# Hand-written table of order: another order, engine choice and set of slots for the same 1,474 nodes

## The chip, the cores and the metric

The kernel runs on one core of a Trainium2 chip. Five engines work side by side: TensorE (PE, with weight loads shown as PEld), VectorE (DVE), ScalarE (ACT), GpSimd (POOL) and SyncE (SP, which here only issues transfers). Each runs its own instructions strictly in order. Sixteen DMA engines move the data that SP, POOL and ACT ask for.

The metric is the device time of one execution in microseconds (us). Before the change it is 289.76 us, the median of three runs (289.59 to 290.92).

## What is computed

Two stages. A linear attention with a feature map of 128 features per sign, for 8 batches, 8 heads, 576 rows and 64 columns a head, and then a feed-forward layer of three products, their maximum, and an output product on 4608 rows:

```python
def phi(x):
    proj = np.einsum('bhsd,df->bhsf', x, w_phi)
    proj = proj - np.max(np.abs(proj), axis=-1, keepdims=True)
    return np.concatenate([np.exp(proj), np.exp(-proj)], axis=-1)
q_p, k_p = (phi(q), phi(k))
kv = np.einsum('bhsf,bhsd->bhfd', k_p, v)
z = np.sum(k_p, axis=2)
num = np.einsum('bhsf,bhfd->bhsd', q_p, kv)
den = np.einsum('bhsf,bhf->bhs', q_p, z)[..., None] + 1e-06
...
h = np.maximum(np.maximum(x @ w1, x @ w2), x @ w3)
return (h @ w_out).astype(np.float32)
```

All inputs and the output are float32 in memory. On the chip the products take bf16.

## The kernel before

**Units.** The attention is cut into 16 units of four heads; two units make one batch. `attention(u)` makes the nodes of one unit, a node being a few instructions of one engine with the nodes that it needs, the buffers that it uses and the function that issues it:

- `L`, `Lv`: loads of q, k and v. Units 0 to 3 load q and k as bf16 through POOL's queue (L449), except for unit 0, whose q and k come in halves as float32 through SP's (L435) and are cast on DVE or ACT (L442). All others load 576 KB each through SP's queue (L460) and are cast on POOL (`C`, L466).
- `T`: q and k of a unit side by side, turned so that columns become partitions (`qkT`). Units 0 to 3 do this on PE with an identity (L480) and copies (`Tc`, L483). Units 4 to 15 do it with one transposing transfer in SP's queue (L495).
- `G`: `psq` and `psk`, the products of `qkT` with the feature weights (L518). They use 64 of PE's rows each, two at a time. Five batches a unit: four of four tiles, one of two. `ek` (ACT, L531) and `r` (DVE, L537) read them.
- `R`, `mT`, `V`: the maxima of q's rows turned on PE (L545), copied (L549), and sent as one more row into `qkT` by a small transfer (L553) from SP's or ACT's queue. Units 0 and 1 do without.
- `M` (L597) and `eq` (L610): the same products for q, transposed, less the maxima, and their exponentials.
- `E`, `va`, `vd` (L568, L572, L582): the exponentials of k's maxima, multiplied into v and beside it.
- `K` (L626): keys by values, 72 matmuls on 64 rows each; `kv` copies the sums (L631). `N` (L644) and `x` (L650, L651): the queries' products and the division.
- `X`: the result turned into `xT`. Units 0 and 1 on PE (L664, L667), the others with a transposing transfer in SP's queue (L674).

**Feed-forward.** `chunk(b, ...)` takes 512 of a batch's 576 rows; a ninth chunk takes the 64 left over from all eight. `up` and `up2` are groups of four matmuls of 512 columns (L697), evacuated by `t1` (ACT L705 or DVE L707) and `h` (DVE L703). `down` is a group of four (L725) and one of six (L730), evacuated by `osb` (L738) into one of four buffers and stored through SP or, in the ninth chunk, ACT (L745). Some nodes at the start prepare products of the weights (`wd`, `wt`, `we`, `wm`, `mo`).

**Order.** Nothing is scheduled while the program is built. `plan` reads a long string, `PLAN`. A word such as `756S0@146.2` says: node 756 goes to SP (T is PE, D is DVE, A is ACT, G is POOL), it takes slot 0 of its buffer, and a planner, which is not part of the kernel, meant it to start at 146.2. The order of the words is the order in which the nodes are issued, so each engine's order follows from it, and the slots say which tile or PSUM bank a node has to wait for.

**Idlers.** The planned starts have one use: where PE's plan has a gap, `fill` puts matmuls into it that use constants and write to a free bank (L827, `idler`).

Of the kernel before, what the change touches and what calls it, by code (L numbers as in the profile page):

```python
# [104 lines left out]
139A@25.0 167D@25.2 165D@25.5 1088T2@25.6 138A@25.6 50G@25.6 1090T1@26.0 124A1@26.1 1089D@26.3 112A@26.3 127G0@26.5 140T5@26.5
70T167@26.7 125G@26.7 1091A@26.8 99D@27.4 111A@27.7 126G@27.9 1096T2@27.9 72D@28.2 141A@28.2 71A@28.5 104D@28.5 142A@28.7
120A@29.3 173T106010@29.3 1097A@29.6 122G@29.6 183T51@29.6 1094T7@29.9 176D@29.9 174A@30.1 187D@30.5 186D@31.1 184A@31.2
73T31@31.3 75T4@31.6 175A@31.7 160D3@31.7 74D1@31.8 128T5@31.9 161S@31.9 1082G@32.1 1095A@32.1 134T6@32.4 362S1@32.4 76D0@32.4
185A@32.6 297S0@32.8 79T2@32.8 135A@33.1 178T47@33.2 80D0@33.4 131T3@33.5 136A@33.7 426S0@33.8 177D@34.0 77T2@34.2 121G@34.2
133A@34.3 1098T6@34.5 181D@34.6 129A@34.8 229D2@35.2 132A@35.3 78D1@35.3 123G@35.3 1080G@35.6 168T01@35.8 182D@35.9 1099A@36.0  # L110
143T032@36.1 171D@36.5 130A@36.5 179A@37.0 172D@37.1 188T60@37.3 231T5@37.4 144A@37.5 192D@37.7 145A@37.8 170A@38.1 191D@38.1
148T20@38.2 232D0@38.4 1092T4@38.5 196A1@38.5 190A@38.7 198G1@38.9 169A@39.0 149D1@39.0 189A@39.5 152T6@39.8 1093A@40.1
83T0@40.1 153D1@40.4 235T5@40.4 180A@40.6 146T4@40.7 197G@41.0 236D@41.0 84A@41.0 81T6@41.1 147D0@41.3 193T5@41.5 150T7@41.5
199A@41.7 233T1@41.8 82A@41.8 194D1@42.0 151D0@42.2 195S@42.3 154T4@42.4 234D@42.8 242T012601@42.8 230S@43.0 365G@43.1 155A@43.1
237T07@43.2 156T5@43.4 245D@43.4 296S1@43.5 238A@43.7 215T143@43.9 157D@44.0 366S1@44.4 246D@44.5 252T51@45.0 241D@45.1
1104T2@45.2 217A@45.2 1083G@45.3 216A@45.5 240D@45.7 253A@45.8 1112T4@46.2 239A@46.3 255D@46.3 1105A1@46.7 256D@46.9 247T03@47.0
1085G@47.4 257T27@47.4 1110T5@47.5 250D@47.6 249A@47.6 248A@48.2 260D@48.2 203T01@48.5 1102T2@48.7 1111A@48.7 251D@48.8
254A@49.2 1081G@49.5 1116T5@49.5 259A@49.7 1103D@49.8 243A@49.9 363S1@50.3 209T1@50.4 205A@50.4 1114T2@50.6 1117D@50.7
557S1@50.7 211A@50.9 261D@51.3 244A@51.4 1124T5@51.5 299G1@51.6 1113D@51.6 204A@51.9 210A@52.3 200T6@52.4 212T4@52.6 1125D@52.6
1122T3@52.7 1084G@52.7 213A@52.9 202A@53.2 1115D@53.2 262T0@53.5 1108T5@53.6 265A1@53.7 1123D@53.8 263A1@53.9 214A@54.1  # L120
264S@54.3 258A@54.4 387T111010@54.5 367T32@54.7 1109A@54.7 429G0@54.8 382T47@54.9 390D@54.9 428S0@55.0 201A@55.2 1120T5@55.3
# [4 lines left out]
392T7@63.1 278T2@63.3 285D@63.3 374A@63.4 222T5@63.5 393D0@63.7 220T1@63.8 430G@63.9 378A@63.9 376D@64.0 394S@64.0 1126T7@64.1
279A@64.4 286D@64.6 298S2@64.7 395A0@64.8 223D1@64.9 272T6@65.0 280A@65.1 275T0@65.2 396G1@65.2 287T40@65.4 273A@65.5 431S0@65.6
1127T@65.7 288D1@66.0 276A@66.0 274A@66.5 221D0@66.6 277A@67.0 307T013201@67.2 397G@67.3 302T46@67.4 1128A1@67.5 289T1@67.6
310D@67.7 291T5@68.0 304A@68.1 305D@68.2 1134T7@68.4 308A@68.5 292D0@68.8 303A@69.0 408T31@69.2 560G1@69.4 1135T@69.5 311D@69.5
226S@69.5 410A@69.7 290D0@70.1 309A@70.2 559G@70.5 409A@70.6 306D@70.7 293T4@70.8 317T12@71.1 1136A3@71.1 294D1@71.3 322T06@71.4  # L130
312T53@71.5 398G@71.6 324A@71.8 1138T7@71.9 320D@71.9 318A@72.1 295S@72.1 325D@72.5 319A@72.6 402T4@72.7 624G0@72.8 316D@72.9
411T1@73.0 1139T@73.1 403A@73.2 315D@73.5 323A@73.7 404A@74.0 491S1@74.0 321D@74.1 414T050@74.4 412A@74.4 326D@74.7 313A@74.7
1140D0@75.0 330A1@75.2 314A@75.4 332G0@75.5 399T2@75.6 416D@75.8 415A@75.9 405T6@75.9 442T003710@76.1 400A@76.1 561S1@76.3
# [725 lines left out]
```

## Time and profile before

| | |
|---|---|
| median of three runs | 289.76 us (289.59 to 290.92) |
| the profiled execution: its time | 290.44 us |
| its span, first to last instruction | 288.7 us |
| granted TensorE clock | 1.000 |
| moved by DMA | 51.45 MB, 178 GB/s on average |
| transposing transfers of `qkT` | 12, SP's queue held 2.7 to 6.2 us each |

A row of the chain of waits gives start, length and what the time went to: an engine with a line of the kernel, or a transfer on which the next instruction waited. A row of a timeline gives start, duration, engine, line, operation and tiles; brackets at its end hold the idle time of the engine just before it and what ended it. A row of the groups has the count, the busy time, the mean duration in ns, and the idle time before the group. A row of the windows gives, behind the stretch and its length, the busy time and the count of PE, PEld, DVE, ACT and POOL, the granted clock, the share of the DMA engines that was busy, and GB/s. PE's matmuls overlap in their pipeline, so the durations of single ones add up to more than the time they take together.

### The profile page before, as it was taken

The page shows a single profiled execution, that of the slowest core. Times are in us where ns is not written, and L with a number is a line of the kernel's source. Part 1 is how long each engine was busy: PE and PEld are TensorE (multiplying, and loading weights), DVE is VectorE, ACT ScalarE, POOL GpSimd, SP SyncE. Part 2 cuts the span into 40 slices and gives each one's busy share as a digit, 9 for nine tenths or more (in the row PEclk, how much of TensorE's full clock was granted, in tenths as well). Part 3 has the DMA queues.
Part 4 walks back from the last instruction along what each step waited for, and adds up shares of the span by engine and source line. Part 5 has one row for each costly group of instructions (what it writes and reads, how often), then busy time and mean ns, then how long its engine had stood idle before and what let it go on. Part 6 is the DMA issues. An engine that isn't in the chain of part 4 may idle for free.

```text
span 288.7 us, 8634 instructions
## 1 busy us (share of the span) xinstructions
PE 279.6 (97%) x3587; PEld 155.0 (54%) x3587; DVE 204.9 (71%) x431; ACT 197.8 (69%) x456; POOL 121.8 (42%) x104
## 2 busy tenths in 40 slices
PE   8999999998999999999998999999999999999994
PEld 3466675465565655556455466565544654444452
DVE  3978888897999787967788778897976362156210
ACT  2799898998989998886896978977664501330021
POOL 8048969949517159564552634062162000000000
PEclk9999999999999999999999999999999999999999
DMA  7999979999989999999999988869400037610064
GB/s 184 275 251 209 236 280 205 283 309 210 178 208 257 254 262 238 246 213 272 209 231 226 257 177 201 210 136 143 82 4 0 2 75 144 139 30 0 6 157 130
DMA packets 68193, 51.45 MB, mean 178 GB/s; under 512 B 48762, under 2 KB 52922, under 8 KB 68154
## 3 DMA queue, kind: packets, MB, share of 16 engines
q1 hardware_dynamic: 63759, 45.55, 66.6%
q0 software_dynamic: 4000, 4.92, 9.9%
q8 instruction: 28, 0.46, 0.7%
q10 hardware_dynamic: 395, 0.43, 0.4%
q14 instruction: 11, 0.09, 0.1%
HBM read 34.64 MB, written 9.44 MB: 153 GB/s over the span
## 4 chain that ended last, share of the span: by engine, by line
PE 75%; DMA 15%; ACT 5%; DVE 2%; SPq 1%; issue 1%; ACTq 0%
PE ups L697 29%; PE ops L730 13%; DMA qkT<-qk_bf 9%; PE ops L725 9%; PE psn L644 5%; PE psq L518 5%; PE kvps L626 4%; PE psm L597 4%; DMA k_raw<-in_k_dram 2%; ACT Eq L610 2%; DMA xT<-x_sb 2%; PE pm L796 2%; ACT Ek L531 2%; DMA qkT<-mT 1%; DVE mqp L537 1%; PE idler L827 1%
## 5 line engine op out<-in xcount | busy, mean ns | idle before, releaser
L697 PE MATMUL ups<-xT,w_bf 128*128 128x512 bf16 x432 | 102.0, 379 | 0.2
L610 ACT ACTIVATE Eq<-psm 128x512 bf16<-128x512 f32 (+1 forms) x160 | 80.4, 575 | 18.6 <-PE psm L597 17.6
L531 ACT ACTIVATE Ek<-psk 128x512 bf16<-128x512 f32 (+1 forms) x160 | 81.8, 574 | 9.8 <-PE psk L518 7.3
L572 POOL TENSOR_TENSOR vab<-v_raw,em 128x1152 bf16<-128x1152 f32 (+1 forms) x35 | 67.2, 1929 | 50.2 <-ACT em L568 44.5
L697 PEld LDWEIGHTS <-w_bf 128*128 128x128 bf16 x432 | 40.2, 98 | 44.7 <-issue 0.4
L537 DVE TENSOR_REDUCE mqp<-psq 128x4 bf16<-128x512 f32 (+1 forms) x80 | 49.0, 633 | 10.8 <-PE psk L518 7.8
L537 DVE TENSOR_REDUCE mk<-psk 128x4 f32<-128x512 f32 (+1 forms) x80 | 49.4, 630 | 4.6 <-PE psk L518 2.7
L730 PE MATMUL ops<-wout_bf,hT 128*128 128x512 bf16 (+1 forms) x222 | 51.5, 373 | 0.0
L703 DVE TENSOR_TENSOR hT<-hT,ups 128x512 bf16<-128x512 bf16 x54 | 35.8, 682 | 11.9 <-PE ups L697 10.0
L738 ACT COPY osb<-ops 128x512 f32<-128x512 f32 (+1 forms) x21 | 12.2, 586 | 30.8 <-PE ops L730 13.4
L651 DVE TENSOR_TENSOR x_sb<-psn,rden 128x320 bf16<-128x320 f32 x64 | 31.5, 492 | 2.2
L644 PEld LDWEIGHTS <-Eq 128*128 128x128 bf16 x640 | 26.8, 97 | 11.4 <-DVE x_sb L651 0.4
L730 PEld LDWEIGHTS <-hT 128*128 128x128 bf16 x222 | 20.8, 98 | 21.2 <-DVE hT L703 0.2
L705 ACT ACTIVATE hT<-ups 128x512 bf16<-128x512 f32 x33 | 19.6, 607 | 18.1 <-PE ups L697 16.9
L644 PE MATMUL psn<-kv_sb,Eq 128*128 128x65 bf16 x640 | 29.3, 194 | 0.3 <-DVE x_sb L651 0.3
L738 DVE COPY osb<-ops 128x512 f32<-128x512 f32 (+1 forms) x16 | 10.7, 670 | 25.4 <-PE ops L730 12.7
L518 PE MATMUL psq<-w,qkT 64*128 64x128 bf16 x288 | 24.1, 217 | 2.7 <-DMA qkT<-qk_bf 2.6
L518 PEld LDWEIGHTS <-qkT 64*128 64x128 bf16 x576 | 16.5, 94 | 16.2 <-issue 9.6
L725 PE MATMUL ops<-xT 128*128 128x512 bf16 x96 | 24.5, 379 | 0.0
L518 PE MATMUL psk<-w,qkT 64*128 64x128 bf16 x288 | 24.1, 217 | 0.0
L466 POOL CAST qk_bf<-k_raw 128x1152 bf16<-128x1152 f32 x12 | 13.7, 1146 | 22.7 <-DMA k_raw<-in_k_dram 22.7
L597 PE MATMUL psm<-qkT,wphi_m 128*128 128x512 bf16 (+1 forms) x70 | 21.8, 358 | 0.3 <-DMA qkT<-mT 0.3
(71 smaller groups left out, 245.2 us busy)
## 6 DMA issues: line engine op xcount, KB each, us to landing
v_raw<-in_v_dram SPq DMA_DIRECT2D x16, 576.0 KB, 5.5
out_dram<-osb SPq DMA_DIRECT2D x65, 128.0 KB, 2.5
q_raw<-in_q_dram SPq DMA_DIRECT2D x12, 576.0 KB, 7.0
k_raw<-in_k_dram SPq DMA_DIRECT2D x12, 576.0 KB, 6.0
w_bf<-in_moe_w_dram POOLq DMA_DIRECT2D x3, 768.0 KB, 14.7
qk_bf<-in_q_dram POOLq DMA_DIRECT2D x3, 288.0 KB, 12.6
qk_bf<-in_k_dram POOLq DMA_DIRECT2D x3, 288.0 KB, 11.9
wout_bf<-in_moe_w_out_dram POOLq DMA_DIRECT2D x1, 768.0 KB, 20.9
```

Source lines behind the costliest of these rows:

```text
L518: nc.tensor.matmul(ps()[:, i, :], lhsT=cols[r, :], rhs=w2[r, c, :], start=True, stop=True)
L531: nc.scalar.activation(Ek[s]()[:, tiles_of(t0, n), :], of(1), EXP, scale=1.0 - 2.0 * s)
L537: nc.vector.tensor_reduce((mq, mk)[c]()[:, tiles_of(t0, n)], of(c), AXX, ALU.max, apply_absolute_value=True)
L572: (nc.vector if n_.eng == "DVE" else nc.gpsimd).tensor_tensor(vab()[:, g, t0:t1, 0:D], vb()[:, t0:t1, :], em()[:, g, t0:t1].unsqueeze(2).t ...
L597: nc.tensor.matmul(psm()[:, 0:w], lhsT=wphi_m, rhs=rhs, start=True, stop=True)
L610: nc.scalar.activation(Eqb()[s][:, cols], psm()[:, 0:w], EXP, scale=1.0 - 2.0 * s)
L644: nc.tensor.matmul(psn()[:, c, :], lhsT=Eqb()[g][:, t0:t0 + P], rhs=kv()[:, pr, ab, g, :], start=(g == 0), stop=(g == 1))
L651: nc.vector.tensor_tensor(x_sb()[:, pr, :, ab, :], psn()[:, :, 0:D], rden().to_broadcast([P, 5, D]), ALU.mult)
L697: nc.tensor.matmul(ups(), lhsT=w_bf[i + 1][:, ct, j * P:(j + 1) * P], rhs=tokens_of(ct), start=(ct == 0), stop=(ct == CT - 1))
L703: nc.vector.tensor_tensor(hT()[:, j, :], hT()[:, j, :], ups(), ALU.max)
L725: nc.tensor.matmul(ops_()[:, 0:width], lhsT=tile_of(ct, tt), rhs=line_w[c_i > MOVE][:, ct, cols], start=(ct == 0), stop=False)
L730: nc.tensor.matmul(ops_()[:, 0:width], lhsT=hT()[:, j, tt * P:(tt + 1) * P], rhs=wout_bf[:, j, cols], start=False, stop=(j == JT - 1))
```

## The change

The string `PLAN` is replaced by another one. All other lines stay: the nodes, what each computes, the dependences, the buffers and their numbers. What differs is the order of the words, the engine letter of 80 nodes (of those that may run on more than one), slots, and the planned starts. The number of idlers in the program goes from 43 to 34. On PE the order changes between matmuls on 64 rows (`G`, `K`) and on 128 rows 75 times before and 81 times after; four of the six more lie ahead of the first `up`.

The words of the nodes that the prediction speaks of, and of some near them:

| nodes | what | words before | words after |
|---|---|---|---|
| 10, 6 | first halves of unit 0's k and q, loads | 10S1@0.7 6S0@1.1 | 10S1@1.1 6S0@0.7 |
| 9, 14 | casts of the second halves of unit 0's q and k | 9A@7.4 14A@9.1 | 9D@6.8 14D@8.6 |
| 361 | load of unit 5's q | 361S0@8.2 | 361S1@2.8 |
| 88 | load of unit 1's v | 88S@14.7 | 88S@24.1 |
| 1087 | copy of the first turned w1 tile | 1087D1@19.0 | 1087A1@18.7 |
| 50, 123 | columns of ones-times-em (`vd`) of units 0 and 1 | 50G@25.6 123G@35.3 | 50A0@17.8 123A@34.3 |
| 195, 589, 784, 914, 979 | `V` of units 2, 8, 11, 13, 14 | 195S@42.3 589S@103.6 784A@169.8 914S@152.7 979S@195.2 | 195A@40.7 589A@103.4 784S@171.4 914A@155.8 979A@210.3 |
| 301, 691, 756 | `T` of units 4, 10, 11 | 301S2@59.7 691S1@117.9 756S0@146.2 | 301S2@58.6 691S0@119.6 756S1@148.0 |
| 719 | `V` of unit 10 | 719S@144.0 | 719S@147.1 |
| 297, 296, 426 | loads of unit 4's k, q and unit 6's q | 297S0@32.8 296S1@43.5 426S0@33.8 | 297S1@38.1 296S1@32.9 426S0@32.0 |
| 1459, 1460, 1463, 1464 | the last full `down` and its copy out | 1459T@280.2 1460A2@281.8 1463T@275.9 1464A1@277.5 | 1459T@278.5 1460D1@280.0 1463T@282.0 1464D2@283.5 |

SP's order around three transposing transfers, before and after (a letter and the unit; `L` is a load of q or k):

```
T4   before: Lv5 L8 V3 Lv6 L9 L8 L6 T4 V5 Lv4 T6
     after:  L8 Lv3 Lv5 V3 Lv6 Lv4 L6 T4 L9 L8 V5 T6
T10  before: store1 store1 X6 store1 Lv9 T10 L11 L11 V9 T13
     after:  store0 store1 V7 X6 store1 T10 Lv9 L12 L11 V9 T13
T11  before: L15 store2 X8 store2 L12 V10 Lv13 T11 L14 V13
     after:  Lv12 L15 L15 X8 Lv13 V10 T11 store2 store2 L12 X9
```

The diff replaces the whole string; these are lines that hold words of the table:

```diff
...
-158G@4.5 1079G@5.2 7A@5.7 1G@6.0 16T5@6.4 1077G@6.5 17D2@7.2 9A@7.4 27T103510@7.9 361S0@8.2 22T27@8.2 30D@8.4 31D@9.0 14A@9.1
...
-115T012701@14.6 88S@14.7 58T30@14.7 118D@15.0 117A@15.0 61T5@15.3 41D@15.3 59A@15.5 64T2@15.8 48D1@15.9 38A@16.0 89T6@16.3
...
+2D7@0.7 4A@0.7 0G@0.7 6S0@0.7 3D@1.1 10S1@1.1 85G1@1.2 8S@1.5 13S@2.0 86G@2.0 15S1@2.4 361S1@2.8 1076G@2.9 7A2@3.6 1G@3.6
...
+1088T1@23.1 163D2@23.2 107A@23.4 67T6@23.6 87D1@23.8 117A@23.9 137T70@24.0 109D@24.0 88S@24.1 101A@24.1 70T134@24.5 1089D@24.6
...
-371D@58.9 266G@59.1 427S0@59.3 208A@59.4 1119D@59.5 301S2@59.7 218T2@59.7 379A@59.9 281T00@60.1 269T7@60.2 219D1@60.3 1131T@60.4
+1107A@58.4 301S2@58.6 391D@58.8 208A@58.9 386D@59.1 377T50@59.3 1100G@59.5 1130T4@59.6 1119D@59.7 383A@59.8 379A@60.3 380D@60.3
...
-628A@117.7 691S1@117.9 637T70@118.0 636D@118.1 544T045@118.4 639A@118.6 640D@118.7 1187A@119.1 631D@119.3 642T27@119.5
+637T04@119.5 651D@119.5 691S0@119.6 1422G@119.7 1187A@119.7 544T056@119.8 640D@120.1 1193A@120.2 641D@120.7 642T21@120.9
...
-667A@143.8 1014G@143.9 1228T0@144.0 719S@144.0 895D@144.2 894A@144.3 883S3@144.7 1244T5@144.8 896D@144.9 1100G@145.0 1229A@145.1
-1235D@145.5 664A@145.6 668T7@145.7 1230T6@145.9 1245D@146.1 669A@146.2 756S0@146.2 670A@146.7 907T23@146.8 739T110@147.0
+666A@145.7 663A@146.1 1235D@146.2 717T1@146.3 1228T3@146.3 1015G0@146.5 667A@146.6 718D0@146.8 888A@147.1 719S@147.1
+907T26@147.2 668T1@147.4 664A@147.6 1014G@147.6 910D@147.6 1230T7@147.7 756S1@148.0 1245D@148.0 670A@148.0 908A@148.5
...
```

More of the change, by code (lines that the diff above doesn't have):

```diff
@@ L105 @@
[L105 to L121, printed above, removed]
@@ L126 @@
[L126 to L133, printed above, removed]
@@ new lines @@
+421T71@85.6 455D@85.6 444A@85.8 1164T6@85.9 493S0@85.9 441D@86.0 1147A@86.2 881S0@86.4 422D0@86.5 439A@86.7 417T5@86.8
+582T113110@87.1 1165D@87.2 334T40@87.3 1156T2@87.6 418D0@87.8 336A@87.9 584A@88.4 343T0@88.5 335A@88.6 340T5@88.7 586D@88.7
+457T7@88.9 423T6@89.0 585D@89.1 342A@89.2 419T4@89.3 458D0@89.4 424D1@89.6 1158T3@89.6 344A@89.7 459S@89.7 495G@90.0 460A1@90.1
+420D0@90.2 345A@90.3 337T7@90.5 1160T6@90.7 1159D@90.8 341A@90.8 425S@91.0 625G2@91.1 338A@91.3 1157D@91.4 346T5@91.5
+1142T0@91.7 583A@91.8 348A@92.0 1161D@92.1 462G0@92.2 339A@92.3 496S2@92.3 572T23@92.5 347A@92.8 577T14@92.8 1143A@93.1
@@ new lines @@
+602A@110.0 882S1@110.1 597T6@110.4 513A@110.5 488T01@110.6 1183D@110.7 1194T1@110.9 604A@111.0 489D1@111.3 598A@111.5
+1141S@111.7 486T5@111.8 511D@111.9 605A@111.9 484T7@112.1 599A@112.4 1184T4@112.4 1195D@112.5 1177S@112.9 525A0@112.9
+485D0@113.1 526G0@113.3 522T3@113.3 606T0@113.3 482T2@113.5 607A@113.7 594T6@113.8 609T117@114.0 483D0@114.0 608A@114.1
+595A@114.3 487D0@114.8 596A@114.9 1188T0@115.2 527G@115.4 1185D@115.4 611A@115.4 610A@115.7 523D0@116.0 627T106710@116.1
+524S@116.4 647T41@116.5 632T25@116.6 630D@116.7 1192T3@116.8 649A@116.8 490S@117.1 633A@117.1 635D@117.3 689G@117.5 648A@117.6
@@ new lines @@
+538T3@124.9 618T40@125.1 1205D@125.1 540A@125.4 532T0@125.4 1206T5@125.6 631D@125.8 534A@125.9 533A@126.5 614T2@126.5
+535T1@126.8 541T6@127.0 612T0@127.1 543A@127.4 652T7@127.5 1207T@127.5 539A@127.7 613D0@127.7 537A@128.1 653D1@128.3 615D1@128.5
+654S@128.7 536A@128.7 1210T0@128.8 619D0@129.1 542A@129.2 886S2@129.4 655A1@129.4 553T21@129.7 657G0@129.8 551T7@130.0
+554D0@130.2 702T006301@130.3 712T41@130.6 1211T@130.7 552D1@130.8 703A@130.9 1208A0@131.3 705D@131.5 656G@131.9 714A@132.0
+547T2@132.1 1209S@132.2 1212A2@132.4 549T7@132.4 548D0@132.7 1218T6@132.8 713A@133.0 704A@133.2 550D1@133.3 659T21@133.6
@@ new lines @@
+1219T@133.9 716D@133.9 819G1@134.0 555S@134.1 660A@134.1 706D@134.3 661A@134.7 715D@134.9 1423G@135.1 658A@135.1 692T71@135.2
+1220A1@135.4 947S1@135.4 707T30@135.5 754G2@135.5 674T025@135.7 695D@135.7 818S2@135.9 693A@136.0 710D@136.3 694A@136.6
+755G@136.6 697T64@136.8 1011S1@136.8 1214T7@137.0 708A@137.1 701D@137.3 711D@137.9 699A@138.0 616T3@138.0 1215T@138.3
+1012S0@138.4 617D0@138.5 709A@138.6 675A@139.0 700D@139.2 1226T3@139.6 696D@139.8 1216A0@139.8 620S@140.0 676A@140.4
+1238T2@140.5 1227A0@140.7 698A@141.2 671T6@141.3 887T115010@141.4 1239D@141.6 673A@141.7 892T71@141.7 720A0@142.0 1222T4@142.0
@@ new lines @@
+741A@150.2 909A@150.5 900D@150.6 733T00@150.6 899A@150.8 1213S@150.8 1224T4@150.8 911D@151.2 735A@151.3 682D0@151.6 679T1@151.7
+903A@151.7 1221S@152.0 1242T6@152.0 734A@152.2 680D0@152.3 904A@152.7 912T7@152.9 1236T0@152.9 1225A@153.2 913D1@153.2
+817S0@153.2 901D@153.4 736T1@153.8 1240T4@153.9 1243D@154.0 950G2@154.1 738A@154.2 737A@154.5 1237D@154.6 683T2@154.8
+915A0@154.8 898A@155.0 1258T6@155.1 917G0@155.2 684D0@155.3 740A@155.5 914A@155.8 748T00@155.9 1241D@156.0 685S@156.1
+772T003201@156.3 762T17@156.6 767T54@156.8 775D@156.8 1259T@157.0 763A@157.1 916G@157.3 749D1@157.4 1217S@157.5 773A@157.5
@@ new lines @@
+764A@158.0 776D@158.1 1254T3@158.4 946S1@158.7 766D@158.7 774A@158.8 753S0@159.1 724T0@159.3 770D@159.3 820G@159.4 1255T@159.5
+726A@159.7 1260D2@159.9 725A@160.3 1426G@160.6 918A@160.8 919T71@160.8 768A@161.0 1250T5@161.0 1256D1@161.1 920A@161.4
+765D@161.7 1257S@161.8 928T0@161.9 769A@161.9 922T6@162.1 727T3@162.3 929A@162.4 771D@162.5 1251T@162.6 921A@162.9 930A@163.3
+728A@163.8 931T7@163.8 925T1@164.0 1252D0@164.1 1264T0@164.2 923A@164.3 821S2@164.4 729A@164.8 1262T2@165.0 924A@165.3
+1265D1@165.3 933A@165.7 777T54@165.9 934T036@166.1 1263A@166.1 781D@166.4 926A@166.6 780D@166.7 779A@167.1 757T20@167.2
@@ L231 @@
+1459T@278.5 1457S@279.1 1462T3@279.8 1460D1@280.0 1471T@280.7 1461S@280.8 1467T@281.3 1472A3@281.6 1463T@282.0 1473A@282.1
+1468D0@282.2 1469S@282.8 1464D2@283.5 1465S@284.3
 """
```

202 lines of the change are left out of this document (98 added, 104 removed).

## The prediction

> **What bounds the kernel now.** I read the page's shares first, then the groups of PE, the chain of waits, and around each long transfer of that chain the timeline of PE and of SP's queue.
>
> ```profile
> span 288.7 us, 8634 instructions
> PE 279.6 (97%) x3587; PEld 155.0 (54%) x3587; DVE 204.9 (71%) x431; ACT 197.8 (69%) x456; POOL 121.8 (42%) x104
> ...
> L827 PE MATMUL idler<-idle 128*128 128x512 bf16 x43 | 14.0, 443 | 1.0 <-DVE idle L400 1.0
> ```
>
> PE is the bound. Only `idler` matmuls (14.0 us) do nothing for the output, so the time can fall only where PE idles or runs idlers: the first stretch, the waits behind it, and the tail.
>
> ```profile
> 9.06 0.67 ACT qk_bf L442
> ...
> 44.89 1.83 PE ups L697 x8
> ...
> 58.29 9.42 DMA qkT<-qk_bf
> ...
> 85.22 0.86 PE ups L697 x4
> ...
> 104.52 4.02 DMA qkT<-mT
> ...
> 120.97 7.83 DMA qkT<-qk_bf
> ...
> 133.96 6.33 DMA xT<-x_sb
> ...
> 148.71 8.81 DMA qkT<-qk_bf
> ...
> 284.74 0.59 ACT osb L738
> ```
>
> Behind the first stretch the chain is PE work, broken by five transfers. These rows, from the timelines at their ends, give PE's idle time in brackets:
>
> ```profile
> 67.76 0.23 PE L518 MATMUL psq<-w,qkT 64*128 64x128 bf16 x1 [1.06 <-DMA qkT<-qk_bf]
> ...
> 108.58 0.59 PE L597 MATMUL psm<-qkT,wphi_m 128*128 128x512 bf16 x2 [0.33 <-DMA qkT<-mT]
> ...
> 128.84 0.23 PE L518 MATMUL psq<-w,qkT 64*128 64x128 bf16 x1 [0.43 <-DMA qkT<-qk_bf]
> ...
> 157.57 0.23 PE L518 MATMUL psq<-w,qkT 64*128 64x128 bf16 x1 [1.11 <-DMA qkT<-qk_bf]
> ...
> L697 PE MATMUL ups<-xT,w_bf 128*128 128x512 bf16 x432 | 102.0, 379 | 0.2
> ```
>
> They are the transposes of units 4, 10 and 11 (2.6 us), the row of maxima of unit 8 (0.3) and, in the last row, the 0.2 us before the `ups` that wait for unit 7's `xT`. Together 3.1 us: all that better timed transposing transfers can win directly.
>
> **The change part by part.** The same nodes run; order, slots, some engines and the idlers differ. *Waits: -3.1 us, with 0.7 us coming back.* A transfer's lead is the PE work between the step that lets it start and its first user. I count it in both orders and price the difference by rows: four `ups` matmuls 0.86 (above) and
>
> ```profile
> 77.13 0.05 PE psq L518
> ...
> 79.52 0.97 PE ups L697 x4
> ...
> 82.49 1.10 PE kvps L626 x72
> ...
> 86.08 0.22 PE psm L597
> ...
> 89.35 0.31 PE psn L644 x10
> ```
>
> A batch of `G` is four such `psq` steps, 0.2. From `R` of unit 3 to the first `G` of unit 4 there are two groups of four 512-column matmuls and one `psm` more: 1.9 us of lead against a wait of 1.06. From the last `N` of unit 6 to `G` of unit 10: one such group, two `N`, one `M`, one `K` and two changes of matmul shape more, 3.0 against 0.43. From `R` of unit 8 to its `M`: `G` batches worth 0.5 and two shape changes more, 0.7 against 0.33. These three waits should go.
>
> Unit 11 goes the other way: from `R` of unit 10 to `G` of unit 11 there are four groups of four, two `G`, two `M` and one `N` fewer, 4.6 us less lead; and `V` of unit 10 loses 6.6 us before its `M`. What offsets it is SP's queue:
>
> ```profile
> 141.62 0.22 PE L545 MATMUL pmT<-ident,mqp 128*128 128x128 bf16 x1
> ...
> 140.87 2.88 SPq L745 DMA_DIRECT2D out_dram<-osb  x2
> 143.84 1.38 SPq L674 DMA_TRANSPOSE xT<-x_sb  x1
> ...
> 146.66 0.54 SPq L460 DMA_DIRECT2D k_raw<-in_k_dram  x1
> 147.30 0.81 SPq L553 DMA_DIRECT2D qkT<-mT  x1
> ...
> 148.71 5.46 SPq L495 DMA_TRANSPOSE qkT<-qk_bf  x1
> ...
> DMA to landing us min/median/max: 5.0/6.3/7.5
> ```
>
> `R` ran at 141.62, yet `V` went out 5.7 us and `T` 7.1 us later, behind stores, a transpose and loads. In the new order X8, one v load, `V`, `T` follow each other, and the stores and the k load that stood ahead come behind the transpose. That returns most of the 4.6 and takes one 576 KB load from in front of it. At the median landing the transpose is early, at 8.81 us late by about 1. `V` of unit 10 keeps 4.3 us from `R` to `M` (two groups of four, two and a half `G`, one each of `M`, `K` and `N`, four shape changes); unit 8's took 4.02 from its issue alone. Unit 7's `X` loses 0.5 us of PE lead, and the k load before it moves. Together nothing to 3.1 us; I take 0.7, since the two largest waits have their cover and only short ones are left open.
>
> [...]
>
> ```profile
> q_raw<-in_q_dram SPq DMA_DIRECT2D x12, 576.0 KB, 7.0
> k_raw<-in_k_dram SPq DMA_DIRECT2D x12, 576.0 KB, 6.0
> ...
> L531 ACT ACTIVATE Ek<-psk 128x512 bf16<-128x512 f32 (+1 forms) x160 | 81.8, 574 | 9.8 <-PE psk L518 7.3
> L738 DVE COPY osb<-ops 128x512 f32<-128x512 f32 (+1 forms) x16 | 10.7, 670 | 25.4 <-PE ops L730 12.7
> ```
>
> *The first stretch: +0.9 us.* Up to the first `ups` (44.89 us) PE has the same work in both orders, but ACT, the busy engine there, doesn't:
>
> ```profile
> 0.00:20.00 20.00, 18.46 (x203) 9.26 (x204) 13.64 (x36) 12.35 (x27) 8.35 (x17) 1.00 0.99 235
> 20.00:40.00 20.00, 19.58 (x412) 13.00 (x408) 16.26 (x37) 18.50 (x44) 15.93 (x17) 1.00 1.15 258
> ...
> L442 ACT CAST qk_bf<-q_raw 128x576 bf16<-128x576 f32 x2 | 1.3, 672 | 4.0 <-DMA q_raw<-in_q_dram 4.0
> L582 ACT CAST vab<-em 128x36 bf16<-128x36 f32 x7 | 2.6, 366 | 0.0
> L785 ACT COPY hT<-pwT 128x1024 bf16<-128x1024 bf16 x1 | 1.0, 1037 | 0.0
> ...
> L553 SPq DMA_DIRECT2D qkT<-mT x13: 759/802/1026, 41.8 to 210.8; - x13
> L553 ACTq DMA_DIRECT2D qkT<-mT x1: 1447/1447/1447, 172.3 to 172.3; - x1
> ```
>
> ACT (fourth busy column) is taken for 18.50 of 20 us. Ahead of the last `xT` copy that the first `ups` need, it gets one `hT` copy (1.04), two `vd` (0.73), one `Ek` (0.57) and the `V` of unit 2 (0.80 by SP's row, 1.45 by ACT's own), and gives two casts (1.34) to DVE: 1.8 to 2.5 us more. PE has four more shape changes there, at 0.1 each (`ups` 0.97 against 0.86). Upper bound 2.5. Lower bound: 43 idlers become 34; if the nine at 0.33 us (14.0/43) are time really saved, -2.9. ACT is nearest to deciding, but has 1.5 us idle in that window and loses the casts before its dense part; so +0.9.
>
> *The rest.* Two more shape changes behind 47 us: +0.2. The last full copy out moves from ACT (0.59) to DVE (0.67): +0.1. The further engine changes (`kv`, `t1`, `mT`, `osb`) are swaps both ways, hidden by PE while ACT and DVE have slack; uncovered each costs one copy, under 0.7.
>
> The sum: -3.1 + 0.7 + 0.9 + 0.2 + 0.1 = -1.2 us. The profiled execution took 290.44 us with a span of 288.7, so 287.5 and 289.2; it lay 0.7 over the runs' median of 289.76. From that median: 288.6 us, 0.4% less.
>
> **The rivals.** *(a) The first stretch gets shorter.* The nine idlers vanish because work reaches PE earlier: -2.9 in place of +0.9, 284.8 us, half of that 286.7. For it: two casts leave ACT, which can start its `Ek` while k's last half (cast at 9.06) is still awaited. Against: the added ACT work, and unit 1's v load, whose gate stands much later in DVE's order.
>
> *(b) An early load crowds out unit 1.* Unit 5's q load takes the other slot and no longer waits for a cast of unit 0: it follows unit 0's v at once, while the 16 engines are 0.99 busy at 235 GB/s (first window). If its 576 KB go before unit 1's q and k, everything in the stretch is 2.5 us late: 291.1, slower. It decides once unit 1's transposes wait over 1.2 us longer. Against it: it stands behind unit 0's four halves and v in SP's queue. [...]
>
> *(c) The gain doesn't come.* The cut leads of `V` 10 and `T` 11 cost the full 3.1 us again, +2.4: 291.0. For it: `T` holds SP 5.46 us and stores queue behind it. Against: the counted leads of units 4 and 10.
>
> *(d) ACT pays for the transfers it now issues.* Four `V` against one before; besides unit 2's, unit 8's and one more are additional. At 1.45 us each, with `Ek` and `Eq` behind them and PE waiting for their banks: +2.9, 291.5, slower. It decides when over 1.2 of the 2.9 us reach PE. For it: ACT's dense stretches. Against: one row alone gives 1.45.
>
> **How the numbers follow.** A change of 0.5% (1.45 us) is about what can be told from none. Forecast 0.46 (its own range 287.4 to 289.8; 0.17 of it below 288.3), (a) 0.14, (b) 0.11, (c) 0.14, (d) 0.15. Faster: 0.17 + 0.14 = 0.31. Slower: 0.06 of (b), 0.04 of (c), 0.13 of (d) = 0.23. Same: 0.46. The range runs from half of (a), 286.6, to between (c) and (d), 291.2.
>
> **What would show it.** Right: no PE idle behind a `qkT` transpose over 0.5 us, 0 to 1 us before unit 10's `psm`; first `ups` 0 to 2 us after 44.89. Wrong: `psq` waits as long as before (c); first `ups` before 44 (a); unit 1's `tps` over 1.2 us later than before (b); PE waiting for `Ek` or `Eq` around unit 8's `V` (d).

## The result, and the profile after

The changed kernel takes 291.75 us (median of 18 runs, 290.40 to 295.28) against 290.02 for the kernel before in the same session (18 runs, 288.89 to 291.99): a ratio of 1.005, 95% interval 1.0029 to 1.0071. It is slower, by 0.8 to 2.1 us. The ratio is of mean times and leaves out the one slow run, 295.28. A second session gave 1.0052 (1.0029 to 1.0075). The forecast of 288.6 was wrong in sign, and 291.75 lies above its range. (The number of nodes that change their engine is 79, not 80.)

Its profiled execution took 292.73 us. The string of the new order has one line more, so each line number is one higher than before (L518 is L519). The first rows of its page, and of its groups on PE:

```profile
span 290.9 us, 8638 instructions
...
PE 278.3 (96%) x3578; PEld 155.2 (53%) x3578; DVE 205.7 (71%) x436; ACT 199.1 (68%) x456; POOL 117.9 (41%) x101
```

```profile
L698 PE MATMUL ups<-xT,w_bf 128*128 128x512 bf16 x432 | 102.2, 379 | 0.0
...
L598 PE MATMUL psm<-qkT,wphi_m 128*128 128x512 bf16 (+1 forms) x70 | 22.6, 358 | 1.3 <-DMA qkT<-mT 1.3
...
L828 PE MATMUL idler<-idle 128*128 128x512 bf16 x34 | 11.5, 450 | 1.0 <-DVE idle L401 1.0
```

PE is busy for 1.3 us less than before (279.6): the idlers take 2.5 us less, and all the rest about 1.2 us more. The span is 2.2 us longer, so PE idles about 3.5 us more. The list of what PE waited for says where (engine, line, what it waited for, us in total, times, longest):

```profile
PE psq L519 <- DVE qkT L484: 2.1, 1, 2.1
PE psm L598 <- DMA qkT<-mT: 1.3, 1, 1.3
PE kvps L627 <- POOL vab L573: 1.2, 1, 1.2
...
PE psn L645 <- issue: 0.6, 1, 0.6
```

No `psq` waits for a transposing transfer any more, as meant: the 2.6 us of units 4, 10 and 11 are gone. The first row lies at 9.73 us, ahead of the last cast of unit 0's k, where idlers stood before. The last row, at 68.60 us, stands in this one profile of the changed kernel and in neither of the two taken later. Further on stand the small row of maxima (`qkT<-mT`, 1.3 where it was 0.3) and unit 1's `K`, which waits for its v. The chain of waits, in order of time, holds both:

```profile
2.11 8.14 DMA k_raw<-in_k_dram
...
34.58 3.38 POOL vab L573 x3
38.00 1.25 PE kvps L627 x70
...
47.60 0.97 PE ups L698 x4
...
91.52 6.91 DMA qkT<-mT
98.47 0.60 PE psm L598 x2
...
286.93 0.69 DVE osb L739
```

The first `ups` of the chain stand at 47.60, 2.7 us later than before (44.89). Part of that lies ahead of the stretch: k's last half of unit 0 was cast at 10.28 here (the row is below) and at 9.06 before. Counted from that cast to the first `ups` record of the timelines (47.53 and 44.83), the stretch takes 37.25 us against 35.77.

For unit 1's `K` the timelines of SP and POOL show the cause. Before:

```profile
14.50 0.37 SPq L460 DMA_DIRECT2D v_raw<-in_v_dram  x1
```

After (the first row joins two loads, unit 1's v at 24.95 and another at 32.15):

```profile
24.95 7.57 SPq L461 DMA_DIRECT2D v_raw<-in_v_dram  x2
```

```profile
33.47 4.48 POOL L573 TENSOR_TENSOR vab<-v_raw,em 128x576 bf16<-128x576 f32 x4 [1.83 <-DMA v_raw<-in_v_dram]
```

In the new words unit 0's and unit 1's v share slot 1, so the second has to wait until unit 0's v has been used: 24.95. POOL waits 1.83 us for it, and `K`, behind POOL, 1.24. For the row of maxima of unit 6 SP's timeline reads, before and after:

```profile
82.25 0.45 SPq L460 DMA_DIRECT2D k_raw<-in_k_dram  x1
82.80 4.08 SPq L745 DMA_DIRECT2D out_dram<-osb  x4
86.93 0.59 SPq L460 DMA_DIRECT2D k_raw<-in_k_dram  x1
87.61 0.79 SPq L553 DMA_DIRECT2D qkT<-mT  x1
```

```profile
88.37 0.59 SPq L461 DMA_DIRECT2D k_raw<-in_k_dram  x1
89.08 0.42 SPq L461 DMA_DIRECT2D v_raw<-in_v_dram  x1
89.60 0.41 SPq L461 DMA_DIRECT2D q_raw<-in_q_dram  x1
91.52 0.80 SPq L554 DMA_DIRECT2D qkT<-mT  x1
92.78 2.23 SPq L675 DMA_TRANSPOSE xT<-x_sb  x1
```

Three loads of 576 KB go out within 1.3 us, and the 4.5 KB behind them take 6.91 us to land. Before, one such load stood 0.7 us ahead of it, four stores of 128 KB and another load further off (5.4 us), and it landed 3.43 us after its issue, too early to be waited for.

### The profile page after: what moved, and what is told of

The parts are those of the page before. It is cut to its first block, busy times and chain, and to the rows that moved or that the text cites. A ratio compares the mean times of both kernels' runs of the same rounds, so it can differ in the third digit from the quotient of the medians.

```text
span 290.9 us, 8638 instructions
## 1 busy us (share of the span) xinstructions
PE 278.3 (96%) x3578; PEld 155.2 (53%) x3578; DVE 205.7 (71%) x436; ACT 199.1 (68%) x456; POOL 117.9 (41%) x101
## 4 chain that ended last, share of the span: by engine, by line
PE 80%; ACT 7%; DMA 5%; DVE 2%; issue 2%; POOL 1%; SPq 0%; DVEq 0%; ACTq 0%; POOLq 0%
PE ups L698 31%; PE ops L731 16%; PE ops L726 10%; PE kvps L627 6%; PE psn L645 6%; PE psq L519 5%; PE psm L598 5%; ACT Ek L532 3%; DMA k_raw<-in_k_dram 3%; DMA qkT<-mT 2%; ACT Eq L611 2%; POOL vab L573 1%; DVE mqp L538 1%; PE pm L797 1%; ACT hT L786 1%
## 5 line engine op out<-in xcount | busy, mean ns | idle before, releaser
L532 ACT ACTIVATE Ek<-psk 128x512 bf16<-128x512 f32 (+1 forms) x160 | 83.3, 574 | 19.4 <-PE psk L519 15.8
L573 POOL TENSOR_TENSOR vab<-v_raw,em 128x1152 bf16<-128x1152 f32 (+1 forms) x36 | 67.9, 1906 | 67.4 <-ACT em L569 43.8
L611 ACT ACTIVATE Eq<-psm 128x512 bf16<-128x512 f32 (+1 forms) x160 | 81.9, 576 | 15.8 <-PE psm L598 15.5
L704 DVE TENSOR_TENSOR hT<-hT,ups 128x512 bf16<-128x512 bf16 x54 | 35.8, 682 | 20.2 <-PE ups L698 16.7
L706 ACT ACTIVATE hT<-ups 128x512 bf16<-128x512 f32 x36 | 21.6, 609 | 27.2 <-PE ups L698 24.1
L645 PEld LDWEIGHTS <-Eq 128*128 128x128 bf16 x640 | 25.7, 97 | 10.3 <-issue 1.0
L645 PE MATMUL psn<-kv_sb,Eq 128*128 128x65 bf16 x640 | 28.0, 194 | 0.6 <-issue 0.6
L519 PE MATMUL psq<-w,qkT 64*128 64x128 bf16 x288 | 24.9, 218 | 2.5 <-DVE qkT L484 2.1
L519 PE MATMUL psk<-w,qkT 64*128 64x128 bf16 x288 | 24.8, 217 | 0.5 <-DVE mqp L538 0.4
L519 PEld LDWEIGHTS <-qkT 64*128 64x128 bf16 x576 | 17.0, 94 | 14.8 <-issue 8.9
L739 DVE COPY osb<-ops 128x512 f32<-128x512 f32 (+1 forms) x17 | 11.4, 672 | 18.0 <-PE ops L731 14.2
L598 PE MATMUL psm<-qkT,wphi_m 128*128 128x512 bf16 (+1 forms) x70 | 22.6, 358 | 1.3 <-DMA qkT<-mT 1.3
L627 PE MATMUL kvps<-vab,Ek 64*128 64x65 bf16 x1152 | 20.2, 190 | 1.2 <-POOL vab L573 1.2
```

The lines of the kernel that those rows point to most:

```text
L519: nc.tensor.matmul(ps()[:, i, :], lhsT=cols[r, :], rhs=w2[r, c, :], start=True, stop=True)
L532: nc.scalar.activation(Ek[s]()[:, tiles_of(t0, n), :], of(1), EXP, scale=1.0 - 2.0 * s)
L573: (nc.vector if n_.eng == "DVE" else nc.gpsimd).tensor_tensor(vab()[:, g, t0:t1, 0:D], vb()[:, t0:t1, :], em()[:, g, t0:t1].unsqueeze(2).t ...
L598: nc.tensor.matmul(psm()[:, 0:w], lhsT=wphi_m, rhs=rhs, start=True, stop=True)
L611: nc.scalar.activation(Eqb()[s][:, cols], psm()[:, 0:w], EXP, scale=1.0 - 2.0 * s)
L627: nc.tensor.matmul(kvps[ab]()[:, t // NT, g, :], lhsT=Ek[g]()[r, t, :], rhs=vab()[r, g, t, :], start=(t + g == 0), stop=(t == UT - 1 and g ...
```

## The experiments

Of the 18 kernels two are the kernel before and two the changed one again; all others change only words of the table (place, slot, engine), so they compute the same. Their line numbers are five higher than those before (L702 is the `ups` of L697), but for the two kernels run again. Ratios are to the kernel before in the same session. In most traces of the experiments some 40 matmul records are missing; waits named below were read at matmuls whose records are there.

The first eight runs set three explanations against each other: the two moved loads of the first stretch (unit 5's q early, unit 1's v late), the work given to ACT there, and the stretch behind 47 us with its small transfers.

**The two loads.** On the new order, unit 5's q load back in the slot that makes it wait; unit 1's v load early in a slot of its own; and both:

```diff
-361S1@2.8
+361S0@7.0
```

> The changed kernel with one word changed: unit 5's q load takes slot 0 again, as before, and so waits for unit 0's cast. Theory L (early loads): the last half of unit 0's k is cast near 9.1 us instead of 10.28, the first G and all behind it up to about 30 us come 1.0 to 1.4 us earlier; unit 1's v is as late as it was, so the wait of K of unit 1 on vab grows from 1.4 to about 2.4 us and the end moves by no more than 0.3 us. Theory A (ACT's added work): the cast moves but ACT's chain does not; the first ups stay at 47.6 us in both theories, but under A the K wait stays 1.4 us. Theory O (the order of the first loads, q before k, is the cause): the cast stays at 10.3 us.

```diff
-87D1@23.8 88S@24.1
+87D3@13.35 88S@13.4
```

> The changed kernel with unit 1's v in slot 3 instead of slot 1, which unit 0's v holds to 24.7 us; its gate and load are issued near 14 us, as before. Theory L: v lands by 23 us, the wait of 1.41 us of K of unit 1 at 38.0 us goes, first ups 1.0 to 1.4 us earlier than 47.60, end 1.0 to 1.4 us earlier (about 0.4%). Theory A: K waits for POOL and ACT instead, the first ups move by less than 0.4 us.

> Both edits of the loads. Theory L: first ups 2.2 to 2.7 us earlier than 47.60, so near 45.0 as in the kernel before; end about 2.4 us earlier, ratio to the kernel before about 0.998. Theory A: first ups not before 46.5 us, ratio above 1.001.

Ratios: q5_late 1.003 (1.0006 to 1.0055), v1_early 1.0003 (0.9965 to 1.0041), both 1.0008 (0.9987 to 1.0030). No cost of the q load shows: putting it back leaves 1.003, with `K` still waiting 1.1 us and the first `ups` 38.3 us behind the cast. The early v load takes `K`'s wait away, yet in its profile the first `ups` come 37.1 us behind the cast of k's last half, hardly sooner. The chain of waits of v1_early shows what has taken the place of POOL and `K`, two `Ek` and a copy on ACT:

```profile
36.41 1.08 ACT Ek L536 x2
37.50 0.49 ACT xT L805
38.03 0.38 PE pm L801
```

PE idles 0.34 us before that `pm` (a product of the weights), and 0.26 inside an `X`. The times of v1_early and of both together lie nearer to the kernel before, with intervals that include it.

**The q load in the old order.** The same word put into the kernel before:

```diff
-361S0@8.2
+361S1@2.8
```

> The kernel before with one word changed: unit 5's q load takes slot 1 and is issued right behind unit 0's v, as in the changed kernel. Theory L: the second halves of unit 0's q and k land 0.5 to 1.2 us later, first ups 0.3 to 1.2 us later than 44.89, ratio 1.001 to 1.004. If SP's queue is served strictly in order: nothing moves, ratio within 0.001 of 1.

Ratio 0.9996 (0.9969 to 1.0023): nothing. Its profile has the order of before around all transposes, yet only one of the three waits, as its list of PE's waits shows:

```profile
PE psq L523 <- DMA qkT<-qk_bf: 1.1, 1, 1.1
```

That is unit 4's. Those of units 10 and 11 did not happen in this execution.

**ACT's work.** On the new order, the `hT` copy, both `vd` and the `V` of unit 2 back on the engines they had:

```diff
-1087A1 50A0 123A 195A
+1087D1 50G0 123G 195S
```

> The changed kernel with the first stretch's added ACT work given back: the copy of the first turned w1 tile to DVE, the two vd of units 0 and 1 to POOL, V of unit 2 to SP. Theory A (ACT's added 1.8 to 2.5 us set the first ups): first ups 0.8 us or more earlier than 47.60. Theory L: less than 0.3 us, since K of unit 1 waits for the v load at 33.4 us however ACT stands.

Ratio 1.0057 (1.0004 to 1.0110), first `ups` 37.4 us behind the cast. Giving ACT's work back alone gains nothing. But unit 1's v is still late here, and `K` waits 0.8 us for it (and 0.2 for a `vd` that POOL now makes), so a delay by ACT that lies behind this wait could not show. No run gives ACT's work back with v early.

**The small transfers.** With both loads as in q5_late_v1_early, either two loads (unit 7's v, unit 13's q) moved from before the `V` of unit 6 to behind it, or the `V` of units 5 and 6 put into ACT's queue:

```diff
-493S0 881S0 ... 459S
+459S 493S0 881S0
```

> The changed kernel with unit 5's q load late, unit 1's v early, and the loads of unit 7's v and unit 13's q moved behind V of unit 6 in SP's queue. If small transfers queued behind loads took the place of the transposes (theory V): PE's wait for V of unit 6 (1.2 to 1.5 us in three of four runs) falls under 0.3 us; waits of psm on qkT<-mT in all under 1.0 us; end 0.8 to 1.2 us earlier than with the two load edits alone, ratio to the kernel before 0.996 to 0.998. Rival W (the wait moves on): V of unit 6 is on time but X of unit 5 or T of unit 7, now behind the two loads, make PE wait as long; ratio 1.000 to 1.002.

```diff
-394S ... 459S
+394A ... 459A
```

> The changed kernel with the two load edits and V of units 5 and 6 issued by ACT's queue instead of SP's. Theory V: their transfers no longer stand behind SP's loads, so waits of psm on qkT<-mT fall from 2.0 to under 0.8 us in all, ratio 0.996 to 0.999. Rival: the DMA engines are shared, the transfers stay 5 to 7 us long and the waits stay between 1.3 and 2.0 us; ratio 1.000 to 1.002.

Both profiles lose the wait: `psm` waits for `qkT<-mT` 0.4 us in the first and none worth a row in the second, against 2.0 in the kernel without the edit. The row of unit 6 landed 2.2 us after its issue with the loads behind it, and 5.3 us after it in ACT's queue. The times do not follow: 1.0031 (1.0006 to 1.0055) and 1.0036 (1.0010 to 1.0061), no better than the 1.0008 of the kernel without the edit in another session.

**Transposes earlier in the old order.** In the kernel before, loads and stores ahead of the transposes of units 4, 10 and 11, of unit 8's row of maxima and of unit 7's `X` moved behind them (the first lines of it):

```diff
-621S1 ... 556S0 ... 301S2 394S 298S2
+301S2 556S0 394S 298S2 621S1
...
```

> The kernel before with its own PE order, but with two loads moved behind T of unit 4, one store behind T of unit 10, a store and a load behind T of unit 11, a load behind V of unit 8 and a load behind X of unit 7. It tells what the waits of 3.1 us are worth without a new order. If they are worth what the prediction's first term says: T, V and X waits of PE fall from 3.1 to under 1.2 us, end 1.5 to 2.5 us earlier, ratio 0.992 to 0.996. If the wait only moves on (moved loads late, POOL's casts and later transposes late): ratio 0.999 or more.

Ratio 1.0042 (1.0013 to 1.0071). The waits that the prediction wanted to remove are gone, but for 0.2 us at unit 4's transpose, and another has come, in PE's timeline:

```profile
79.22 0.39 PE L702 MATMUL ups<-xT,w_bf 128*128 128x512 bf16 x1 [1.21 <-DMA xT<-x_sb]
80.28 1.02 PE L702 MATMUL ups<-xT,w_bf 128*128 128x512 bf16 x4 [0.67 <-DMA xT<-x_sb]
```

The loads that left the transpose alone now stand before unit 3's `xT`. The kernel before had no wait at those `ups`.

**Both kernels again.** To see which waits belong to the order, and which to one execution, both were profiled twice more, unchanged.

> The kernel before, unchanged, to see what of its profile repeats. Theory V (its waits of units 4, 10 and 11 come from how long the transfers took in one execution): 0 to 3 of the three waits come back, their sum anywhere in 0.5 to 3.5 us and not 2.6 again; k's last half is cast anywhere in 7.8 to 10.4 us, first ups 35.5 to 36.5 us behind it. Theory O (the waits belong to the order): the same three waits, 1.1, 0.4 and 1.1 within 0.3 us each.

> As before_again: V, another sum of the three waits than before_again and than 2.6; O, 2.6 again within 0.6.

> The changed kernel, unchanged. Theory V: no wait over 0.5 us behind the transposes, a wait of 0.5 to 2 us for the row of maxima of one or two of units 5, 6 and 8, not always the same; first ups 36.8 to 38.3 us behind the cast of k's last half. Theory O: unit 6's row of maxima costs 1.5 us again and unit 1's K 1.2 us again, first ups at 47.5.

> As after_again: V, another set of waits for rows of maxima; O, the same waits again.

The waits of PE for the transposes in the two new profiles of the kernel before (from the list of waits, and the rows in the timeline), the first of them

```profile
PE psq L518 <- DMA qkT<-qk_bf: 1.8, 2, 1.2
```

```profile
68.71 0.23 PE L518 MATMUL psq<-w,qkT 64*128 64x128 bf16 x1 [1.23 <-DMA qkT<-qk_bf]
...
157.20 0.23 PE L518 MATMUL psq<-w,qkT 64*128 64x128 bf16 x1 [0.59 <-DMA qkT<-qk_bf]
```

and the second

```profile
PE psq L518 <- DMA qkT<-qk_bf: 2.5, 2, 1.3
```

```profile
69.40 0.23 PE L518 MATMUL psq<-w,qkT 64*128 64x128 bf16 x1 [1.31 <-DMA qkT<-qk_bf]
...
174.42 0.23 PE L518 MATMUL psq<-w,qkT 64*128 64x128 bf16 x1 [1.24 <-DMA qkT<-qk_bf]
```

Unit 4's wait returns each time (1.06, 1.23, 1.31, and 1.1 in b_q5_early). Unit 10's never returns, unit 11's once at half its size, and the last row is unit 12's, which the prediction had not seen. The sums 1.8 and 2.5 look like the 2.6 of the first profile; what they are made of is different.

The same lists for the changed kernel, first after_again,

```profile
PE psm L598 <- DMA qkT<-mT: 1.3, 1, 1.3
...
PE kvps L627 <- POOL vab L573: 1.0, 1, 1.0
```

then after_again_2:

```profile
PE kvps L627 <- POOL vab L573: 1.0, 1, 1.0
PE psm L598 <- DMA qkT<-mT: 0.9, 1, 0.9
```

The wait for a row of maxima is there each time, though not always at the same unit: before unit 6's `psm` in two profiles (at 98.47 and 96.38), before unit 5's in the other (at 71.99). `K` waits for v each time. So both belong to the new order. The cast that the whole start hangs on, in the changed kernel's first profile and in one of the kernel before:

```profile
10.28 0.46 DVE L443 CAST qk_bf<-k_raw 128x576 bf16<-128x576 f32 x1 [0.60 <-DMA k_raw<-in_k_dram]
```

```profile
10.03 0.67 ACT L442 CAST qk_bf<-k_raw 128x576 bf16<-128x576 f32 x1 [1.00 <-DMA k_raw<-in_k_dram]
```

In us; the column "of one execution" is the profiled one's own time:

| profile | cast of k's last half | first `ups` behind it | PE waits for transposes | for rows of maxima | `K` for v | of one execution |
|---|---|---|---|---|---|---|
| before | 9.06 | 35.8 | 2.6 | 0.3 | 0 | 290.44 |
| before_again | 9.89 | 35.7 | 1.8 | 0.2 | 0 | 290.07 |
| before_again_2 | 10.03 | 36.2 | 2.5 | 0.2 | 0 | 291.36 |
| after | 10.28 | 37.3 | 0 | 1.3 | 1.2 | 292.73 |
| after_again | 9.49 | 37.1 | 0 | 1.3 | 1.0 | 290.67 |
| after_again_2 | 9.64 | 37.0 | 0 | 0.9 | 1.0 | 290.63 |

In before_again and before_again_2 the record of the very first `ups` is missing: their rows hold seven where the profile before has eight, behind 0.16 us of seeming idle time. The table takes the start of the missing one, 0.15 us behind the last matmul ahead of it, as in the profile before.

A second reading follows PE along the span. The durations of PE's groups are added up in the order of issue (four `ups` 0.86, a `K` 1.10, and so on), and for equal sums the time since the cast of k's last half is compared with that of the profile before (us more; the heads are the times in that profile):

| | 62 | 68 | 105 | 160 | end |
|---|---|---|---|---|---|
| before_again | 0.0 | +0.1 | +0.2 | -1.2 | -1.2 |
| before_again_2 | +0.4 | +0.7 | +0.7 | -1.4 | -0.1 |
| after | +1.6 | +1.2 | +3.0 | +0.9 | +0.9 |
| after_again | +1.4 | +0.3 | +1.7 | -0.3 | -0.3 |
| after_again_2 | +1.3 | +0.2 | +1.5 | -0.6 | -0.5 |

With the means of three and three (the profile before counts as 0): up to 62 us the new order loses 1.3, wins 1.0 at unit 4's transpose, loses 1.5 between 68 and 105 us, wins 0.9 up to 160 us where units 10 and 11 stand, and 0.4 behind it, where one execution of the kernel before had unit 12's wait. It ends 0.5 us behind, and at 0.7 with the later cast (9.80 against 9.66 on average) and the longer tail.

**Halves joined.** The orders were cut at the first `up` and at 68 us, where the same nodes but a few have been issued in both, and joined crosswise; slots of the second half were renumbered so that no buffer is taken early.

> New order up to the first ups, old order behind it. If the start costs (theory S): 1.0 us and more above before, ratio 1.003 to 1.005; first ups 36.8 to 37.3 us behind the cast of k's last half, and unit 4's wait of 1.1 to 1.4 us still there. If the rest costs (theory R): ratio 0.999 to 1.002.

> Old order up to the first ups, new order behind it. Theory S: 0.3 to 1 us below before, ratio 0.996 to 0.999; first ups 35.8 to 36.4 us behind the cast of k's last half, no wait for unit 4's transpose, 0.9 to 1.5 us for the row of maxima of unit 5 or 6. Theory R: ratio 1.003 to 1.005.

> Old start, new order behind it, and four loads (for units 5, 7, 9 and 13) moved from before the rows of maxima of units 5 and 6 to behind them. Theory S: no wait over 0.5 us for a row of maxima or a transpose, 1 to 2 us below before, ratio 0.993 to 0.997. Theory R: 1.000 to 1.003. If the wait only moves to the loads: a new wait of PE of 0.5 us or more for data of units 7 to 10.

> Old order for the first 394 nodes (to 68 us), new order behind. From the progress of PE in the profiles the new order stands 0.3 to 0.9 us behind at 68 us, and loses about 0.3 to 0.5 more by the rows of maxima of units 5 and 6 less the transposes of units 10 and 11. Theory S (only the start costs): ratio 0.997 to 1.001. Theory R (the rest costs): 1.002 to 1.005, with a wait of 0.9 to 1.5 us for the row of maxima of unit 5 or 6 in the profile.

> New order for the first 394 nodes, old order behind. Theory S: ratio 1.002 to 1.005, first ups 36.8 to 37.4 us behind the cast of k's last half, no wait for unit 4's transpose. Theory R: ratio 0.999 to 1.001.

Ratios, in that order: 1.0028 (0.9998 to 1.0058), 1.0054 (1.0027 to 1.0081), 1.0093 (1.0055 to 1.0131), 1.0100 (1.0063 to 1.0138) and 1.0109 (1.0074 to 1.0144). At 68 us either combination is slower than both kernels it is made of, so the runs cannot divide the loss between the halves: the joins bring waits that neither kernel has. In old_to_68_new_rest one copy out holds PE up for 2.0 us,

```profile
PE psq L523 <- DVE osb L743: 2.0, 1, 2.0
PE psm L602 <- DMA qkT<-mT: 1.0, 1, 1.0
```

and in old_start_new_rest PE loses 1.0 us to `mqp` right behind the join. Nor do their waits repeat cleanly. new_start_old_rest has 2.7 us for transposes, and old_to_68_new_rest has 1.0 for a row of maxima, in the second row above. But old_start_new_rest has neither a wait for a transpose nor one for a row of maxima and takes 1.0054 all the same; and new_to_68_old_rest, with the old order behind 68 us, waits for no transpose, but 1.6 us for rows of maxima and 2.5 for two `K`.

**One wait alone.** In the kernel before, the q loads of units 8 and 9 moved behind unit 4's transpose (node 556 is unit 8's q, not its k), and unit 9's cast moved with its load:

```diff
-621S1@55.4 ... 556S0@56.1 ... 301S2@59.7 ... 394S@64.0
+301S2@59.7 ... 394S@64.0 556S0@64.0 ... 295S@72.1 621S1@72.1
-624G0@72.8
+624G0@77.9
```

> The order before, with two loads that unit 8 and 9 need (k of unit 8, q of unit 9) moved from before unit 4's transpose to behind it, and unit 9's cast behind unit 4's v products. If the wait of 1.1 to 1.4 us can be had alone: it is under 0.3 us, no new wait over 0.5 us, ratio 0.995 to 0.998. If it moves on: a new wait of PE of 0.7 us or more before 90 us (unit 5's row of maxima, xT of unit 3, or unit 4's K), ratio 0.999 to 1.003.

Ratio 1.0198 (1.0152 to 1.0245). Unit 4's wait shrinks to 0.3 us in PE's timeline, but two q loads then take SP 6.60 us, and unit 8's transpose behind them is late:

```profile
75.17 6.60 SPq L465 DMA_DIRECT2D q_raw<-in_q_dram  x2
81.87 4.12 SPq L500 DMA_TRANSPOSE qkT<-qk_bf  x1
```

```profile
89.67 0.28 PE L523 MATMUL psq<-w,qkT 64*128 64x128 bf16 x1 [4.98 <-DMA qkT<-qk_bf]
```

The first of the two loads is unit 9's, the second takes the same slot and waits until unit 9's q has been cast, as POOL's and SP's rows show:

```profile
80.23 1.14 POOL L471 CAST qk_bf<-q_raw 128x1152 bf16<-128x1152 f32 x1 [0.21 <-DMA q_raw<-in_q_dram]
```

```profile
81.40 0.37 SPq L465 DMA_DIRECT2D q_raw<-in_q_dram  x1
```

The cast that I moved ends at 81.37 and the load goes out at 81.40, so this is a price of my edit. It shows what such a move can cost, and not that unit 4's wait can't be had in another way.

## Why the prediction was wrong

**What held.** The waits behind `qkT` transposes did go: none in three profiles of the new order, as "no PE idle over 0.5 us" asked. Unit 4's 1.06 us was counted rightly. The first stretch was forecast 0.9 us longer, and is 1.2 longer behind the cast of k's last half (37.1 against 35.9, means of three). The longer tail was forecast at 0.1: the last copy takes 0.69 on DVE against 0.59 on ACT.

**The step that failed** is "-3.1 us, with 0.7 us coming back". Three things were wrong in it.

The 3.1 was read from one execution as if every wait in it belonged to the order. Only unit 4's 1.1 to 1.3 us and unit 8's 0.2 to 0.3 return whenever the kernel before is profiled. Units 10 and 11 gave 1.54 in the first profile, 0.59 and 0 in the next two (then with 1.24 of unit 12), and 0 in b_q5_early. Of the 0.2 put down to unit 7's `xT`, 0.1 stands there, at 140.33 us, and the rest at 205.09, behind a reduction on DVE. What could be won was some 2.5 us on average (2.9, 2.0 and 2.7 with unit 8's row).

The 0.7 was set for unit 11's transpose and unit 10's `V`, whose leads were cut. Neither waited. What came instead is 0.9 to 1.3 us in every profile, at the `V` of unit 5 or 6, whose neighbours in SP's queue the prediction did not look at: it followed the long transfers and not the 4.5 KB ones that the loads were pushed in front of. With the 0.2 to 0.3 us that such rows cost before, the exchange of one kind of wait for the other leaves 1.4 us (2.3 + 0.2 - 1.2, from the table) where the prediction booked 2.4.

That is 1.0 of the 2.7 us between the forecast (-1.2) and the times (+1.5, interval 0.8 to 2.1); the first stretch adds 0.3. The cause of the rest stays open. The exchange (-1.4) and the first stretch (+1.2) nearly cancel, yet the profiles leave the new order 0.7 us behind on average and the times 1.5. Three profiles a side, whose own times spread by 1.3 and 2.1 us, can't place the difference, and no run here did: where the waits for rows of maxima were taken away, the time did not fall.

**The first stretch: near in size, cause open.** The prediction laid it on ACT. In the three profiles of the changed kernel the chain runs through `K`, which waits 1.0 to 1.2 us for a v whose load was put 10 us later by a shared slot. The prediction had this in view ("unit 1's v load, whose gate stands much later") and put no price on it. That this wait makes the stretch longer is not shown, though: in the four kernels with v early the first `ups` still come 36.8 to 37.1 us behind the cast, and there the chain runs through ACT, as in the rows of v1_early. Taking one of the two away leaves the other, and ACT's work was given back only with v late (act_back 1.0057). Kernels of the new order with v early took 1.0003, 1.0008, 1.0031 and 1.0036 of before, those without 1.0030, 1.0050, 1.0052 and 1.0057. That points to about half of the loss, with intervals that touch and from several sessions; the profiles don't show where it is won.

The first `ups` came 2.7 us later, outside "0 to 2". 1.2 of it is the later cast of unit 0's k, which varies from 9.06 to 10.03 among the three profiles of the kernel before, and on average is 0.1 later in the changed kernel; it can't be put down to the order.

**The rivals.** (a), a shorter first stretch, did not come. (b) fell: the early q load alone gives 0.9996. (d) fell: `V` holds ACT 0.7 to 1.3 us, not 1.45, and PE waits for no `Ek` or `Eq` around unit 8's. Its 291.5 is the nearest to the 291.75 measured, by luck. (c), "the gain doesn't come", gives 291.0, and by its own mechanism it is wrong too, since neither `V` 10 nor `T` 11 waited. The landings in the prediction's rows, 7.83 to 9.42 us for the transposes that delayed PE, 7.0 for q loads and 6.0 for k loads in the median, are of unlike sizes: the loads carry 576 KB, a transposing transfer 288 KB by the kernel's shapes (128x1152 bf16). In the changed kernel the transposing transfers land 4.6 to 8.5 us after their issue, v and q loads after 5.7 and 7.1 in the median. What differs most is the hold: 2.7 to 5.0 us of SP's queue each, where a 576 KB load holds it 0.4 to 0.8.

In the one profile that has the row of maxima in another queue than SP's (loads_and_v_on_act) it landed hardly sooner: unit 6's row after 5.3 us in ACT's queue, against 5.3 to 6.9 in SP's in four profiles (6.91, 5.34, 6.47, and 6.87 in v1_early). In SP's queue with the loads behind it, it took 2.2 (loads_and_v6_first).

No version tried beats the kernel before.

## What to carry to other kernels

Before a wait is booked as a gain, profile the unchanged kernel two or three times: a wait that doesn't return is no property of the order, and a list of waits with the same total can hide different ones. Where transfers are reordered in a queue, count every one that a load is moved in front of, the smallest too. When one wait is cut out of a dense plan, look for what stands next in line: here it came back at another transfer (b_moved, before_t4_first) or on another engine (v1_early), and where no new wait was found (the two kernels with the row of maxima freed) the time did not fall.

## What was not expected of the hardware

A 4.5 KB transfer landed 1.9 us after its issue behind two stores of 128 KB (unit 4's row of maxima in the changed kernel, at 85.97 us) and 2.2 us with the loads moved behind it (loads_and_v6_first), and 5.3 to 6.9 us after it behind three loads of 576 KB. In ACT's queue, in one profile (loads_and_v_on_act), it still took 5.3.

The last half of unit 0's k, among the first transfers of the program, was cast at 9.06, 9.89 and 10.03 us in the three profiles of the kernel before, and the first `ups` follow it there by 35.7 to 36.2 us.
